# Second modulation's broadcasts made in column tiles and spread by DMA, a new order of the dense work, and two batches of the head's matmuls moved

## The chip, the core and the metric

The kernel runs on one core of one Trainium2 chip. The metric is device time in microseconds (us) for one execution of the whole program. A core has TensorE (PE in the profile: matmuls, with weight loads as PEld), VectorE (DVE), ScalarE (ACT), GpSimd (POOL) and SyncE (SP), each of which takes its own instructions in order; nearly all DMAs of this kernel are issued from SP's queue.

## The reference

One transformer-like block with adaptive layer norm. `c` gives six vectors of 512; the first three modulate the attention half, the last three the token-mixing half. Shapes: S = 2048 tokens, D = 512, 32 heads of 16, window 256, F = 1792.

```python
mod = (_silu(c) @ w_mod).reshape(c.shape[0], 6, 1, -1)
sa, ca, ga, sb, cb, gb = (mod[:, n] for n in range(6))
h = _layernorm(x) * (1 + ca) + sa
x = x + ga * A(h, wqkv, wo)          # causal attention, window 256, then @ wo
h = _layernorm(x) * (1 + cb) + sb
x = x + gb * B(h, w1, b1, w2, b2)    # layernorm, then an MLP over the 2048 tokens:
                                     # gelu(h^T @ w1 + b1) @ w2 + b2, transposed back
```

(`...copy()` and the batch dimension of 1 are left out.)

## The kernel before

Tokens are handled in 16 blocks of 128, four blocks to a token group (tg 0 to 3). There are three stages.

*Head* (first exponential at 12.54 us). x and the first third of `w_mod` are loaded; four blocks are normalised (`ln1_apply`, L258) and turned by PE into PSUM banks of pool `hpt` (`turn`, L544; banks for 128-column chunks `dc` 0/2 and 1/3). `fm(k)` (L530) is a batch of eight one-column matmuls that gives the scale and shift of the first modulation; `fm(0, 1, 2)` stands between `turn(1)` and `turn(2)`, `fm(3)` after `turn(3)`. DVE adds 1 (`modFM`, L556), and ACT and DVE modulate from PSUM into `h1T` (L562, L564), in two column parts. Then the first q and k are made (L579, L583, L587).

*Attention* (12.5 to 158.9 us). 76 units (tg, g8, ui): g8 is one of four groups of eight heads, ui a piece of the window (four pieces in tg 0, five after). Each unit has two exponentials on ACT (`emit_exp`, L649), which read scores that PE makes (L626, masks L638). When a (tg, g8) is through, PE multiplies by the values (`emit_av`, L666, reading `VaugT` and its half-swapped copy `Vx`), and DVE and POOL normalise (L677 to L701). Between these stand the *dense groups*, each of four 512-column matmuls and an evacuation on DVE: `q..`, `k..` (L354), `v..` (L331), `wo..` (attention output, L421), `bias`, and `bc..` (the broadcasts, L396). Names carry the token group and head group (`k10`: tg 1, g8 0) or the block (`v6`). Where a dense group is not ready, PE makes partial sums of the MLP's first product (`part_group`, L462), which the last stage then need not make. Only two PSUM banks (`ps_dn`) serve all of these.

The order is decided when the program is built: class `Plan` keeps a clock for each engine with fixed costs for each step (`g.us`, `cost`, `issue(t, cost)` for SP), takes the first name in the string `ORDER` that is ready by that clock, and emits instructions accordingly (`run_dense`, `force`, `drain`, `fill`). `force(needs(u + 1))` makes sure that q and k of the next unit are emitted before its scores. `PLAN` holds six margins. `at_unit` issues one background load per unit (`loads`): `w_mod` for the later modulations, `wo`, zeros for two of the k buffers, then `w1`.

For k of g8 2 and 3 (`copied`), DVE writes a plain copy `k`, and eight small DMAs (L378) put it into the zeroed `KT`. Values are swapped by two DMAs per pair of blocks (`swap`, L322). `h1T` of tg 1 to 3 is turned by DMA (`dma_start_transpose`, L310) and modulated in SBUF. Every DMA shares SP's queue.

The second modulation's vectors (and `ga`) are needed on all 128 partitions: `bc_group(v, ...)` multiplies `sT_rep` (silu of c, repeated over 128 columns, L593) by 512 columns of `w_mod`, four matmuls for each of the four vectors, and DVE casts each into its own tile (L403, L405). After `bc_ga`, four `fold_wod` (L957) multiply it into `wo`. `wo` groups need the folds, `bc_cb1` and `bc_sb`.

*Tail* (158.9 us to the end). `sum_up` (L1106) finishes six of the 14 F-chunks, the last four blocks get `wo` (`t_wo`, L1127) and the second modulation (t1 to t3, blocks `hb` 12 to 15; ACT L1145, DVE L1135 to L1154), L1203 finishes the other eight chunks, and L1227 is the second product `py`, 252 matmuls, with its epilogue.

Of the kernel before, what the change touches and what calls it, by code (L numbers as in the profile page):

```python
# [1 line left out]

# [6 lines left out]
DT = mybir.dt  # L9
# [3 lines left out]
P = 128  # L13
S = 2048
D = 512
# [13 lines left out]
def kernel(  # L29
# [63 lines left out]
    bc_cb1 = const.tile([P, D], DT.bfloat16, name="bc_cb1")  # L93
    bc_sb = const.tile([P, D], DT.bfloat16, name="bc_sb")
    bc_gb = const.tile([P, D], DT.bfloat16, name="bc_gb")
# [4 lines left out]
    bc_ga = modw.tile([P, D], DT.bfloat16, name="bc_ga")  # L100
# [27 lines left out]
    sT_rep = modw.tile([P, ND, P], DT.bfloat16, name="sT_rep")  # L128
# [199 lines left out]

    def v_group(tg, tl):
        def mm(pv, dc):  # L330
            nc.tensor.matmul(  # L331
                pv[:], lhsT=h1T[tg][:, dc, tl * P : (tl + 1) * P],
                rhs=wqkv[:, dc, 2 * D : 3 * D], start=(dc == 0), stop=(dc == ND - 1),
            )

        def evac(pv):
            nc.vector.tensor_copy(
                out=v_heads(tg % 3, tl, 0, H)[:, :, 0:DH], in_=pv[:].rearrange("p (h d) -> p h d", d=DH),
            )
# [8 lines left out]
    def qk_group(tg, g8, kind):  # L348
# [10 lines left out]
        def evac(pq):  # L359
            if kind == "q":  # L360
                QT[tg][g8] = qpool.tile([P, 4 * P], DT.bfloat16, name=f"QT{g8}")
                nc.vector.tensor_copy(out=QT[tg][g8][:], in_=pq[:])
                return
# [24 lines left out]
            ND, mm, evac, 1.35 if masked else 0.65,  # L388
# [5 lines left out]
    def bc_group(v, dst, add1, then=()):  # L394
        def mm(ps_b, k):
            nc.tensor.matmul(  # L396
                ps_b[:], lhsT=sT_rep[:, k, :], rhs=wmod_of(v)[:, k, :],
                start=(k == 0), stop=(k == ND - 1),
            )

        def evac(ps_b):
            if add1:
                nc.vector.tensor_scalar_add(out=dst[:], in0=ps_b[:], scalar1=1.0)  # L403
            else:
                nc.vector.tensor_copy(out=dst[:], in_=ps_b[:])  # L405
        return Group(ND, mm, evac, 0.65, [("w", v)] + [("w", "o")] * (v == 2), ("bc", v), then=then)
# [86 lines left out]
    with tc.manual_schedule():  # L493

        with tc.tile_pool(name="modps", bufs=1, space=bass.MemoryType.PSUM) as modps, tc.tile_pool(
            name="hpt", bufs=2, space=bass.MemoryType.PSUM
# [10 lines left out]
            st_ps = modps.tile([P, ND], DT.bfloat16, name="st_ps")  # L507
            nc.tensor.transpose(st_ps[:], c4[:], identity[0:ND, 0:ND])
# [9 lines left out]
            nc.scalar.activation(out=sig[:], in_=st_ps[:], func=ACT.Exp, scale=-1.0)  # L518
# [5 lines left out]
            nc.vector.tensor_tensor(out=sT[:], in0=st_ps[:], in1=sig[:], op=ALU.mult)  # L524
# [14 lines left out]
            banks = [hpt.tile([P, 2, 4 * P], DT.bfloat16, name="dn") for _ in range(2)]  # L539
            pts = [banks[dc % 2][:, dc // 2, :] for dc in range(ND)]  # L540

            def turn(tl):
                for dc in range(ND):
                    nc.tensor.transpose(  # L544
                        pts[dc][:, tl * P : (tl + 1) * P], xn1[0, tl][:, dc * P : (dc + 1) * P], identity[:]
                    )

            turn(0)
# [3 lines left out]
            fm(0, 1, 2)  # L552
# [5 lines left out]
            def modulate(dc, c0, c1, act):  # L558
                out, src = h1T[0][:, dc, c0:c1], pts[dc][:, c0:c1]
                scale, shift = modFM[:, 4 + dc : 5 + dc], modFM[:, dc : dc + 1]  # L560
                if act:
                    nc.scalar.activation(out=out, in_=src, func=ACT.Identity, bias=shift, scale=scale)  # L562
                else:
                    nc.vector.tensor_scalar(out=out, in0=src, scalar1=scale, scalar2=shift, op0=ALU.mult, op1=ALU.add)  # L564
# [28 lines left out]
            nc.gpsimd.tensor_copy(out=sT_rep[:], in_=sT[:].unsqueeze(2).to_broadcast([P, ND, P]))  # L593
# [112 lines left out]
        def ln23(tb):  # L706
# [21 lines left out]
            def modulate(by, op):  # L728
                return lambda eng: eng.tensor_tensor(out=v["h2"][:], in0=v["h2"][:], in1=by[:], op=op)
# [10 lines left out]
        BC = ((2, bc_ga, False), (4, bc_cb1, True), (3, bc_sb, False), (5, bc_gb, False))  # L740

        def bc(v, dst, add1):
            return bc_group(v, dst, add1, [
                (lambda g=g: fold_wod(g), 0.33, 0.1, ("fold", g)) for g in range(ND)
            ] if v == 2 else ())
# [4 lines left out]
            v1 k20 wo3 q31 v2 q10 q22 k21 q33 wo11 wo6 v0 q02 wo0 q21 k11 q30 k10 bc2 v3 k01 v7  # L750
            v6 v15 wo8 q01 q20 bias k33 q32 v10 k13 wo7 wo9 q03 v4 v8 q11 v5 k02 wo5 k12 v9 k31
            v14 q23 bc3 v13 wo2 k30 bc0 q13 v12 wo10 k22 v11 bc1 wo1 q12 wo4 k32 k23 k03
        """

        def make(name):
            kind, n = name.rstrip("0123456789"), name.lstrip("abciokqsvw")
# [6 lines left out]
            return bc(*BC[int(n)]) if kind == "bc" else bias_group()  # L763

        dense = [make(name) for name in ORDER.split()]
        PLAN = (0.2, 8.0, 5.0, 0.4, 0.6, 0.2)
# [9 lines left out]
        ready["w", "b"], pl.sp = 8.0, 5.0  # L776
# [51 lines left out]
        def drain():  # L828

            while pl.urgent:  # L830
# [3 lines left out]
                pl.dve = max(pl.dve, at) + cost  # L834
# [24 lines left out]
        def step():  # L859
# [5 lines left out]

            def then():
                if g.gives:
                    if g.lag:
                        evens.add(g.gives)
                        both = [("k", g.gives[1], n) for n in (2, 3)]  # L870
                        if all(k in evens for k in both):
                            ready[both[0]] = ready[both[1]] = ready[both[0][:2]] = issue(pl.dve, g.lag)
                    else:
                        ready[g.gives] = pl.dve + 0.1
                    kind, *_, tb = g.gives if g.gives[0] == "v" else ("", 0)
                    if kind:
                        if ("v", tb ^ 1) in ready and (tb % 4 < 2 or tb < 8):
                            ready["vx", tb ^ 1] = ready["vx", tb] = issue(pl.dve, 1.3)
                if g.then:
                    add_chain(g.then, pl.dve + (PLAN[2] if g.then[0][3] else 0.1))  # L880
            pl.urgent.append((pl.pe + 0.2, g.cost, b, g.evac, then))
# [74 lines left out]
        def fold_wod(g):  # L956
            nc.vector.tensor_tensor(out=wod[:, g, :], in0=wod[:, g, :], in1=bc_ga[:], op=ALU.mult)  # L957

        def at_unit(tg, ul, u, t):
# [45 lines left out]
        end, scored, pl.pe = 0.0, 0.6, 0.4  # L1005
# [13 lines left out]
        for u, (tg, g8, ui) in enumerate(units):  # L1019
            half = lambda v: 0.06 + 0.00166 * columns(units[v][0], units[v][2])  # L1020
            emit_exp(u, 0)
            start = max(end, scored)
            end = start + 2 * half(u)
# [14 lines left out]
            due(u + 1, end)  # L1038
            until = end if late or u + 1 in values_at else end - 1.3 if u == last else max(end, scored) + half(u + 1) + 0.1
            run_dense(until)  # L1040
            emit_exp(u, 1)
            if late:
                pl.pe = max(pl.pe, end + 0.05)
                emit_scores(u + 1, (1,))
                pl.pe += 0.37
                until = max(end, scored) + half(u + 1) + 0.1
# [11 lines left out]
        emit_av(NG - 1, ND - 1, (4,), False, True)  # L1058
        norm_out(0)
# [61 lines left out]
    with tc.tile_pool(name="xp2", bufs=4) as xp2, tc.manual_schedule():  # L1121
# [28 lines left out]
        def t2(tb):  # L1150
            h2 = hb[tb]
            t_apply(h2[:], xres[tb][:], (2, tb))
            nc.vector.tensor_tensor(out=h2[:], in0=h2[:], in1=bc_cb1[:], op=ALU.mult)
            nc.vector.tensor_tensor(out=h2[:], in0=h2[:], in1=bc_sb[:], op=ALU.add)  # L1154
# [118 lines left out]
```

## Time and profile before

| what | value |
|---|---|
| median of three runs | 248.73 us (248.49 to 249.42) |
| the profiled execution | 249.06 us, of which its span 247.3 us |
| granted TensorE clock | 1.00 in every stretch |
| head, 0 to 12.5 us | PE busy 9.52, DVE 9.08, ACT 3.59 |
| tg 0, 22.7 to 44.0 us | 21.3 us: ACT busy 20.92, DVE 19.69, PE 18.76 |
| first half of tg 1, 44.0 to 65.4 us | 21.4 us: ACT busy 18.61, PE 19.64, DVE 18.33 |
| 65.4 to 158.9 us | 93.5 us: ACT busy 92.91, PE 90.66, DVE 83.64 |
| start of the tail, 158.9 to 182.8 us | 23.9 us: PE busy 23.90, DMA 395 GB/s |
| last product, 182.8 to 247.3 us | 64.5 us: PE busy 61.56 |

A row of busy times by stretch is read against the stretch's length: an engine whose busy time equals it is what the stretch waits for. In the attention stage that is ACT, in the tail PE. "Busy" of PE counts overlapping matmuls once.

### The profile page before, as it was taken

Reading aid. Unit: us, or ns where it says so; the run is one execution under the profiler, and the core shown is the slowest. Engines: PE = TensorE matmul, PEld = TensorE weight load, DVE = VectorE, ACT = ScalarE, POOL = GpSimd, SP = SyncE. Lnnn points to the kernel's source line nnn. Section 1 sums busy time; section 2 is a strip of 40 time slices with the busy share of each in tenths; the row PEclk is TensorE's granted clock in tenths of the full one; section 3 lists DMA queues with packets and bytes.
Section 4 is the critical chain, followed back from the end, with each engine's and each line's share of the span. In section 5 each row is a group of like instructions: output and inputs, shape, how many; then the busy total and the mean of one; then the engine's idle time right before and its main releaser. Section 6 shows DMA issues by size and latency. Waiting matters only on the chain.

```text
span 247.3 us, 8336 instructions
## 1 busy us (share of the span) xinstructions
PE 233.0 (94%) x3599; PEld 119.7 (48%) x3599; DVE 180.4 (73%) x359; ACT 160.0 (65%) x183; POOL 109.6 (44%) x230
## 2 busy tenths in 40 slices
PE   6898897998899999899999999999999999999995
PEld 2643644544545545545545545544444444444444
DVE  6797999987799798989899999879724404241544
ACT  2395999997899999999999999713574400000000
POOL 6625551217647638875867888537600000000000
PEclk9999999999999999999999999999999999999999
DMA  6977994153640244000239500499970000201031
GB/s 192 332 243 184 160 297 149 24 133 67 178 155 5 52 88 87 11 3 3 52 64 302 159 3 5 150 357 415 409 310 0 0 0 5 82 21 64 24 106 44
DMA packets 32121, 30.49 MB, mean 123 GB/s; under 512 B 16212, under 2 KB 26708, under 8 KB 32084
## 3 DMA queue, kind: packets, MB, share of 16 engines
q1 hardware_dynamic: 32076, 29.96, 40.5%
q8 instruction: 28, 0.46, 0.8%
q14 instruction: 9, 0.07, 0.1%
q10 hardware_dynamic: 8, 0.00, 0.0%
HBM read 22.03 MB, written 2.10 MB: 98 GB/s over the span
## 4 chain that ended last, share of the span: by engine, by line
PE 58%; ACT 26%; DVE 9%; SPq 3%; issue 1%; POOL 1%; DMA 1%; ACTq 0%; POOLq 0%
ACT et L649 26%; PE py L1227 20%; PE pu L1106 8%; PE pss L626 6%; PE pu L1203 5%; PE dn L354 4%; PE dn L331 4%; PE dn L462 4%; SPq L378 3%; PE pss L638 2%; DVE ln_stats L242 2%; DVE KT L384 2%; PE pa L1127 1%; PE dn L421 1%; PE pss L666 1%
## 5 line engine op out<-in xcount | busy, mean ns | idle before, releaser
L649 ACT ACTIVATE et<-pss 128x1024 bf16<-128x1024 f32 (+1 forms) x152 | 139.6, 1039 | 7.0 <-PE pss L638 6.6
L1227 PE MATMUL py<-guT,w2r 128*128 128x512 bf16 (+2 forms) x252 | 48.6, 355 | 0.0
L626 PE MATMUL pss<-QT,KT 32*128 32x64 bf16 (+3 forms) x720 | 37.4, 254 | 4.4 <-ACT et L649 2.1
L1227 PEld LDWEIGHTS <-w2r 128*128 128x128 bf16 x252 | 23.6, 98 | 25.2
L1234 DVE SCALAR_TENSOR_TENSOR o<-py,bFM,bc_gb 128x512 bf16<-128x512 f32 (+2 forms) x18 | 11.9, 687 | 30.0 <-PE py L1227 30.0
L354 PE MATMUL dn<-h1T,wqkv 128*128 128x512 bf16 x120 | 32.6, 381 | 0.5 <-DVE KT L384 0.5
L626 PEld LDWEIGHTS <-KT 32*128 32x128 bf16 x720 | 14.3, 92 | 34.2 <-issue 22.5
L223 POOL TENSOR_SCALAR ln_ve<-ln_mv 128x1 f32<-128x1 f32 (+2 forms) x40 | 9.2, 230 | 41.1 <-DVE ln_mv L243 18.6
L677 DVE STREAM_TRANSPOSE t<-pss 128x512 f32<-128x512 f32 x32 | 20.9, 691 | 5.3 <-PE pss L666 5.3
L666 PE MATMUL pss<-et,VaugT 64*32 64x320 bf16 (+4 forms) x720 | 20.9, 253 | 1.1 <-ACT et L649 0.6
L666 PE MATMUL pss<-et,Vx 64*32 64x320 bf16 (+4 forms) x720 | 21.0, 254 | 0.7 <-DMA Vx<-VaugT 0.7
L693 POOL TENSOR_TENSOR merge<-t,zr 128x512 bf16<-128x512 f32 x13 | 13.8, 1059 | 15.7 <-DVE zr L690 15.7
L638 PE MATMUL pss<-mask_rown,mask_hown 32*128 32x128 bf16 (+1 forms) x304 | 20.7, 206 | 0.0
L666 PEld LDWEIGHTS <-VaugT 64*32 64x32 bf16 x720 | 18.9, 91 | 3.8 <-issue 3.3
L638 PE MATMUL pss<-mask_rfar,mask_hfar 32*128 32x64 bf16 (+1 forms) x304 | 19.9, 200 | 0.0
L226 POOL TENSOR_TENSOR ln_rb<-ln_ve,mhalf 128x1 f32<-128x1 f32 x32 | 18.4, 574 | 2.7
L666 PEld LDWEIGHTS <-Vx 64*32 64x32 bf16 x720 | 17.9, 91 | 2.2 <-DMA Vx<-VaugT 0.9
L331 PE MATMUL dn<-wqkv,h1T 128*128 128x512 bf16 x64 | 17.0, 381 | 1.0 <-DVE KT L384 0.9
L1114 DVE TENSOR_TENSOR gelu_a<-pu,part 128x512 f32<-128x512 f32 x10 | 6.4, 685 | 12.5 <-PE pu L1203 8.2
L462 PE MATMUL dn<-hb,w1hi 128*128 128x512 bf16 x56 | 15.1, 381 | 0.0
L354 PEld LDWEIGHTS <-wqkv 128*128 128x128 bf16 x120 | 9.6, 97 | 10.3 <-DVE KT L384 0.7
L421 PE MATMUL dn<-wod,OTd 128*128 128x512 bf16 x48 | 12.6, 381 | 0.0
(131 smaller groups left out, 368.3 us busy)
## 6 DMA issues: line engine op xcount, KB each, us to landing
w2r<-in_B_w_dram SPq DMA_DIRECT2D x14, 512.0 KB, 10.2
wmod<-in_w_mod_dram SPq DMA_DIRECT2D x12, 256.0 KB, 4.4
w1b<-in_B_w_dram SPq DMA_DIRECT2D x6, 448.0 KB, 5.9
Vx<-VaugT SPq DMA_DIRECT2D x16, 147.5 KB, 2.5
x<-in_A_x_dram SPq DMA_DIRECT2D x16, 128.0 KB, 4.6
w1hi<-in_B_w_dram SPq DMA_DIRECT2D x6, 320.0 KB, 5.0
out_dram<-otile SPq DMA_DIRECT2D x15, 128.0 KB, 1.7
wqkv<-in_B_w_dram SPq DMA_DIRECT2D x4, 320.0 KB, 3.3
```

What stands on the lines that cost most here:

```text
L226: nc.gpsimd.tensor_tensor(out=r, in0=ve[:], in1=mhalf[:, 0:n], op=ALU.pow)
L331: nc.tensor.matmul(pv[:], lhsT=h1T[tg][:, dc, tl * P : (tl + 1) * P], rhs=wqkv[:, dc, 2 * D : 3 * D], start=(dc == 0), stop=(dc == ND - 1),)
L354: nc.tensor.matmul(pq[:], lhsT=wqkv[:, dc, col0 : col0 + P], rhs=h1T[tg][:, dc, :], start=(dc == 0), stop=(dc == ND - 1),)
L421: nc.tensor.matmul(pa[:], lhsT=OTd[tg][g][:, tl * P : (tl + 1) * P], rhs=wod[:, g, :], start=(g == 0), stop=(g == ND - 1),)
L462: nc.tensor.matmul(ps[:], lhsT=w1_of(s0 + n, fc), rhs=hb[s0 + n][:], start=(n == 0), stop=(s0 + n + 1 == s1),)
L626: nc.tensor.matmul(pss[j // 2][:, j % 2, 64 * at : 64 * (at + c1 - c0)], lhsT=Kring[kh // 8 % 3][rows, g8, kh % 8].rearrange("p n t -> p ( ...
L638: nc.tensor.matmul(o[:, at[0] : at[-1] + 1 : step, :], lhsT=mask_h[name][rows].rearrange("p n t -> p (n t)"), rhs=mask_r[name][rows, :].un ...
L649: nc.scalar.activation(out=state["e", tg, g8, ui][:, 2 * a : 2 * a + 2, 0:n], in_=state.pop((u, a))[:, :, 0:n], func=ACT.Exp, scale=SCORE_ ...
L666: nc.tensor.matmul(state["po"][32 * j : 32 * j + 32, par, 64 * c0 : 64 * c1], lhsT=v[:, h * DV : h * DV + 32], rhs=state["e", tg, g8, ui][ ...
L677: nc.vector.transpose(out=state["t2"][:, par, :], in_=state["po"][:, par, :])
L1106: nc.tensor.matmul(pu[fc][:], lhsT=w1_of(sc, fc), rhs=hb[sc][:], start=(sc == done.get(fc, 0)), stop=(sc == NT - 1),)
L1227: nc.tensor.matmul(pys[n][:, c0:c1], lhsT=w2r[:, fc, tb * P : (tb + 1) * P], rhs=guT[fc][:, c0:c1], start=(fc == gelus[0]), stop=(fc == ge ...
```

## The change

1. One `bc` group in place of four. Its four steps each issue four matmuls of 32 columns of weights, one per vector, at `tile_position=(0, 32n)`; the four results land on partitions 32n of one PSUM bank. One DVE instruction adds 1 to the rows of `cb` and casts; one DMA takes partitions 0, 32, 64 and 96 to a DRAM tile `bc_rows`, a second one spreads that to `bc_all` on all partitions. `sT_rep` shrinks to 32 columns per chunk. Two small memsets on POOL are new. The group needs all of `w_mod` (and `wo`) and comes once; the folds follow it.
2. The planner: SP's cost of a load is 1.0 in place of 0.6; start values and margins of `PLAN` differ; a group with `PLAN[6]` could be evacuated on ACT, but `PLAN[6]` is empty, so no instruction moves there. Loads left at the end of the units are issued in one go.
3. `ORDER` is new throughout. The groups of tg 0 come as v0 v1 q01 v3 v2 k01 k02 q02 k03 q03 (before: v1 v2 v0 q02 v3 k01 q01 bias q03 k02 k03). The first ones of tg 1 come as v4 v7 q10 v5 k10, then `bc`, k11 v6 q11 k12 k13 (before: bc0, q10 k11 k10 bc2 v7 v6 k13 v4 q11 v5 k12). As built, `part_group` has 84 matmuls (before 75), `sum_up` 80 (88), the last chunks 60 (61).
4. In the head, `fm(0, 1)` goes ahead of `turn(0)`, and `fm(2)` stays between `turn(1)` and `turn(2)`. The pool `hpt` has a third bank, which takes the first three blocks of chunk 3, so that chunks 1 and 3 no longer share a bank there. The transposed `c` uses one of the three in place of a bank of its own.

```diff
-    sT_rep = modw.tile([P, ND, P], DT.bfloat16, name="sT_rep")
+    sT_rep = modw.tile([P, ND, 32], DT.bfloat16, name="sT_rep")
+
+    bc_row = modw.tile([P, D], DT.bfloat16, name="bc_row")
+    add_row = modw.tile([P, 1], DT.float32, name="add_row")
+    nc.gpsimd.memset(add_row[:], 0.0)
+    nc.gpsimd.memset(add_row[32:64, :], 1.0)
...
-    def bc_group(v, dst, add1, then=()):
+    BC = (2, 4, 3, 5)
+
+    def bc_group(then):
+
         def mm(ps_b, k):
-            nc.tensor.matmul(
-                ps_b[:], lhsT=sT_rep[:, k, :], rhs=wmod_of(v)[:, k, :],
-                start=(k == 0), stop=(k == ND - 1),
-            )
+            for n, v in enumerate(BC):
+                nc.tensor.matmul(
+                    ps_b[32 * n : 32 * n + 32, :], lhsT=sT_rep[:, k, :], rhs=wmod_of(v)[:, k, :],
+                    start=(k == 0), stop=(k == ND - 1), tile_position=(0, 32 * n), skip_group_check=True,
+                )
 
         def evac(ps_b):
-            if add1:
-                nc.vector.tensor_scalar_add(out=dst[:], in0=ps_b[:], scalar1=1.0)
-            else:
-                nc.vector.tensor_copy(out=dst[:], in_=ps_b[:])
-        return Group(ND, mm, evac, 0.65, [("w", v)] + [("w", "o")] * (v == 2), ("bc", v), then=then)
+            nc.vector.tensor_scalar_add(out=bc_row[:], in0=ps_b[:], scalar1=add_row[:])
+            dma.dma_start(out=bc_rows[:], in_=bc_row[0:P:32, :])
+            dma.dma_start(out=bc_all[:], in_=bc_rows[:].unsqueeze(0).to_broadcast([P, 4, D]))
+        return Group(ND, mm, evac, 0.65, [("w", v) for v in BC] + [("w", "o")], ("bc",), us=0.27, then=then)
...
-            banks = [hpt.tile([P, 2, 4 * P], DT.bfloat16, name="dn") for _ in range(2)]
-            pts = [banks[dc % 2][:, dc // 2, :] for dc in range(ND)]
+            banks = [hpt.tile([P, 2, 4 * P], DT.bfloat16, name="dn") for _ in range(3)]
+
+            def pt(dc, c0, c1):
+                n = 2 if dc == 3 and c1 <= 3 * P else dc % 2
+                return banks[n][:, dc // 2, c0:c1]
...
+            fm(0, 1)
             turn(0)
             ln1_apply(0, 3)
             build_masks()
             turn(1)
-            fm(0, 1, 2)
+            fm(2)
             turn(2)
             turn(3)
             fm(3)
...
-            v1 k20 wo3 q31 v2 q10 q22 k21 q33 wo11 wo6 v0 q02 wo0 q21 k11 q30 k10 bc2 v3 k01 v7
-            v6 v15 wo8 q01 q20 bias k33 q32 v10 k13 wo7 wo9 q03 v4 v8 q11 v5 k02 wo5 k12 v9 k31
-            v14 q23 bc3 v13 wo2 k30 bc0 q13 v12 wo10 k22 v11 bc1 wo1 q12 wo4 k32 k23 k03
+            v0 v4 wo7 k20 v7 k32 v12 wo5 q31 q10 v5 bc wo2 v1 wo6 v10 k21 k10 wo10 q01 v3 v2 k30
+            k22 v9 q20 wo8 k01 k23 k11 wo1 v8 v6 wo0 wo4 q33 q30 wo3 v11 q32 v15 q11 k02 v14 q23
+            wo11 q21 q22 k12 k13 q02 k03 q12 q03 k31 v13 k33 bias wo9 q13
...
-        PLAN = (0.2, 8.0, 5.0, 0.4, 0.6, 0.2)
+        PLAN = (0.2, 8.0, 3.0, 0.8, 0.0, 0.2, ())
...
-        ready["w", "b"], pl.sp = 8.0, 5.0
+        ready["w", "b"], pl.sp, pl.dve = 8.0, 5.6, 1.4
...
+                    if g.gives == ("bc",):
+                        issue(pl.dve, 0.65)
+                        pl.sp += 2.0
+                        landed = issue(pl.dve, 0.65) + 0.5
+                        for v in BC:
+                            ready["bc", v] = landed
+                        add_chain(g.then, ready["bc", 2])
+                        return
...
-                ready[key] = issue(t, 0.6) + 1.0
+                ready[key] = issue(t, 1.0) + 1.0
```

More of the change, by code (lines that the diff above doesn't have):

```diff
@@ L864, in step @@
                 return
+            over = pl.pe + 0.2
             def then():
@@ L1004 @@
         last = len(units) - 1
-        end, scored, pl.pe = 0.0, 0.6, 0.4
+        pl.end, pl.half, scored, pl.pe = 0.0, None, 0.6, 0.4
         values_at = {}
@@ L1021 @@
             emit_exp(u, 0)
-            start = max(end, scored)
-            end = start + 2 * half(u)
+            start = max(pl.end, scored)
+            pl.half, pl.end_of = start + half(u), half(u)
+            pl.end = start + 2 * half(u)
             if u == 0:
@@ L1058 @@
         emit_av(NG - 1, ND - 1, (4,), False, True)
+        while loads:
+            o, i, key = loads.pop(0)
+            dma.dma_start(out=o, in_=i)
         norm_out(0)
```

77 lines of the change are left out of this document (44 added, 33 removed).

## The prediction

> **What bounds the kernel now.** I read four views: busy time by stretch, the chain of work that ended last, what the exponentials (ACT, L649) waited for, and SP's queue around the longest such wait. Busy time by stretch first (columns: PE, PEld, DVE, ACT, POOL, granted clock, DMA share, GB/s):
>
> ```profile
> 22.70:44.00 21.30, 18.76 (x459) 10.47 (x457) 19.69 (x37) 20.92 (x25) 8.33 (x14) 1.00 0.79 188
> 44.00:65.40 21.40, 19.64 (x401) 10.05 (x408) 18.33 (x35) 18.61 (x20) 9.00 (x16) 1.00 0.35 75
> 65.40:158.90 93.50, 90.66 (x2059) 49.25 (x2067) 83.64 (x159) 92.91 (x100) 67.81 (x114) 1.00 0.28 77
> 158.90:182.80 23.90, 23.90 (x201) 11.21 (x186) 16.44 (x37) 8.95 (x12) 10.95 (x28) 1.00 1.02 395
> ```
>
> From 65.4 to 158.9 us ACT is busy 92.91 of 93.50: the attention stage cannot end earlier than its exponentials allow, so PE time saved there buys nothing by itself; it can only be spent on partial sums, which shorten the tail. In the tail PE has no gap. ACT has room only before 65.4. The chain of waits names where (start, length, what):
>
> ```profile
> 8.62 0.47 PE dn L544 x8
> 9.09 0.19 PE ps_fm L530 x8
> 9.31 0.18 DVE modFM L556
> 9.51 1.75 DVE h1T L564 x5
> ...
> 20.10 1.41 DVE KT L384 x2
> 21.51 0.61 DVE QT L362
> 22.16 0.40 PE pss L626 x8
> 22.56 0.14 PE pss L638 x8
> 22.70 6.79 ACT et L649 x8
> ```
>
> ACT's timeline gives the size of each wait in brackets:
>
> ```profile
> 12.54 7.16 ACT L649 ACTIVATE et<-pss 128x1024 bf16<-128x1024 f32 x8 [0.26 <-PE pss L638]
> 22.68 20.91 ACT L649 ACTIVATE et<-pss 128x1024 bf16<-128x1024 f32 x24 [2.98 <-PE pss L638]
> 43.98 14.86 ACT L649 ACTIVATE et<-pss 128x1024 bf16<-128x1024 f32 x16 [0.38 <-PE pss L638]
> 60.61 3.77 ACT L649 ACTIVATE et<-pss 128x1024 bf16<-128x1024 f32 x4 [1.78 <-PE pss L638]
> 65.40 1.02 ACT L649 ACTIVATE et<-pss 128x1024 bf16<-128x1024 f32 x1 [1.01 <-PE pss L638]
> ```
>
> So ACT loses 2.98 us at unit 4 (22.68), 0.38 at unit 16, the first of tg 1 (43.98), 1.78 and 1.01 at units 24 and 26 (60.61, 65.40). The last two are SP's: its queue runs without a gap from 47.4 to 66.3 us:
>
> ```profile
> 47.37 2.53 SPq L310 DMA_TRANSPOSE h1T<-xn  x2
> 49.99 1.17 SPq L322 DMA_DIRECT2D Vx<-VaugT  x2
> 51.26 2.56 SPq L310 DMA_TRANSPOSE h1T<-xn  x2
> 53.91 1.18 SPq L322 DMA_DIRECT2D Vx<-VaugT  x2
> 55.20 8.12 SPq L378 DMA_DIRECT2D KT<-k  x8
> ```
>
> The last `Vx` lands at 58.75 and the values' matmuls start at 58.80; the last k copy lands at 64.96 (issued 62.71), the exponential starts 0.44 later. Two of the eight issues took 1.84 us, the others some 0.6; both fell on an instruction fetch.
>
> **Part by part.** Each term is in us of ACT's or PE's path; the profiled run (249.06 us, span 247.3) lies 0.33 over the median of 248.73, and I apply the differences to the median.
>
> *A, the head: −0.55.* The chain goes turn(3), `fm(3)`, `modFM`, `h1T`. `fm(0, 1)` leaves the place ahead of turn(2): 16 of the 24 matmuls that take 0.58 there, 0.39 us. It runs earlier, where PE idles for `xn` (sT is done at 6.75, the block of turn(0) at 7.27). turn(3) cannot start before its own `xn` at 8.24; then 0.47 + 0.19, so `modFM` at about 8.9 in place of 9.31, −0.4. The third bank adds a little: ACT waits 0.61 for DVE's `h1T` (10.18 to 10.79) because chunks share a bank; without it QT is copied earlier, but DVE's own five h1T and six KT steps remain: −0.15. Bounds −0.3 (the bank gives nothing, 8.24 slips by 0.1) and −0.7.
>
> *B, unit 4: −0.6.* There `k01` (two evacuations, 1.41) and then `q01` (0.61) stand between PE and the scores. In the new order q01 comes before k01, with as many groups ahead of them; q01's evacuation then lies beside k01's matmuls and 0.61 leaves the chain. Bounds −0.6 and 0 (DVE late by another step).
>
> *C, unit 16: +1.3.* `k10` was fourth among the first groups of tg 1 with bc0, q10, k11 ahead; now v4, v7, q10, v5 are ahead. Its evacuation (1.41) and the scores (0.54) follow. One more group is 4 × 0.216 = 0.86 of PE and one more evacuation 0.68 on DVE, and v4 to v7 need `h1T` of tg 1; 0.86 to 1.54 of it shows, less what PE is earlier by A and B no longer hides. I take +1.3 between +0.7 and +1.9. A and B are about given back here.
>
> *bc itself.* PE: 16 matmuls at 4.5/16 = 0.28 busy, 0.216 a piece when streamed, 3.45 us; now 16 of 32 columns, four beside each other. The nearest row is the values' matmuls (64*32 tiles), of which eight with 320 columns start within 58.80 to 58.95, the time of one: four passes of 0.216, 0.9 us. 2.6 us of PE is freed, and goes to partial sums. Four casts of 0.69 on DVE become one, −2.1 of DVE in a stage where it has 1.6 to 3.1 spare: worth nothing by itself. SP gains two issues and a hold: the second DMA waits for the first to land. Stores of 64 to 128 KB land 1.5 to 1.7 after issue, so SP is held about 1.6, and everything behind it: one zeroing load, four transposes (1.27 each), the last `Vx`, the k copies, w1hi. Bounds of the hold: 1.5 (those stores) and 6.0 (the zeroing loads, 256 KB, which shared the engines with wmod). I take 1.6, as 4 KB is nearer to the stores. The folds wait for `bc_all`: nothing but `wo` waits for them, half a unit group later.
>
> [...]
>
> *D, units 24 and 26: −1.3.* In the new order SP reaches bc's evacuation at about 44.4 us; 0.6 of issue, 1.6 hold, 0.6 of issue, 0.7 zeroing, 4 × 1.27, 1.2 for Vx: 54.0, where the k copies could start, 1.2 before 55.20. By DVE they start as late as 55.20 + 1.3 (C) − 0.86 (one group fewer ahead of k12) = 55.6. From 54.8: seven issues of 0.65, one or two long ones (+1.25 each), 2.25 to land: 62.9 to 64.1; + 0.44, against 65.40: −2.0 to −0.9 at that point, middle −1.45, of which A, B, C make +0.15; that would be −1.6. I take −1.3, since Vx's wait (1.78) also hangs on v-evacuations that C delays. Bounds −2.8 (both waits go) and +0.6 (as late as before and C in full).
>
> *E, 65 to 159 us: +0.5.* The w1hi and wqkv loads of the late partial sums were issued at 129.4, behind tg 3's k copies (122.3 to 128.0), and landed by 133.4; the changed order makes sums of eight matmuls a chunk from unit 63 on, and four Vx and eight copies stand ahead of their loads. ACT has 0.59 to lose in this stretch now; 0 to +1.2.
>
> *F, the tail: −1.3.* `sum_up` and the last chunks issue 80 + 60 matmuls in place of 88 + 61: 9 × 0.216 = −1.94. But block 15's modulated rows must be there for them: ACT ends it at 180.56, and PE first needs it at 182.77 − 6 × 0.216 = 181.47, a slack of 0.9. With 1.94 gone PE would ask at 179.5; a leftover step of DVE (0.41 at 166.07) disappears from that chain, so it is ready at 180.15: 0.65 of the 1.94 is lost. Bounds −1.94 and −0.9.
>
> Sum: −0.55 − 0.6 + 1.3 − 1.3 + 0.5 − 1.3 = −1.95: **246.8 us**, own range 245.8 to 247.9.
>
> **Rivals.**
> - *The full gain*: q10 and k10 meet a PE already early, C is 0.7, E is 0, F −1.94, D −1.3: −0.55 − 0.6 + 0.7 − 1.3 − 1.94 = −3.7, 245.0. For it: DVE loses three casts. Against: k10 is plainly behind more v groups.
> - *New waits take it back*: C 1.9, E 1.2, B −0.3: −0.55 − 0.3 + 1.9 − 1.3 + 1.2 − 1.3 = −0.35, 248.4. For it: ACT is the bound to 0.6 us over 93.5, so every new wait there counts in full.
> - *Slower: SP held by the round trip through DRAM.* bc_rows is issued right behind a zeroing load; if it lands like that load, 6.0 after issue, the hold is 4.4 longer, the transposes of tg 1, Vx and the k copies are that much later, and the last copy lands at 63.5 + 4.4 − 0.8 (start by SP's 54.0 in place of 54.8) = 67.1; + 0.44 is 2.1 past 65.40. D is then +1.95 in place of −1.3: 250.1; with v7's and k11's groups late as well (h1T of tg 1 by as much), up to 251. It decides from the point where D passes +0.65, a hold some 2.7 longer, 4.3. Against: the stores.
> - *The column tiles do not overlap*, and bc takes up to 3.45 of PE just before tg 1's k11 and v6: C + 1.9, and 2.6 us (12 matmuls) fewer partial sums are possible in the same time: 246.8 + 1.9 = 248.7. Against it: the values' matmuls. [...] No row of the profile has four tiles with all 128 rows.
>
> **How the numbers follow.** Forecast 0.42; full gain 0.15; new waits 0.21; SP held 0.17; no overlap 0.05. What a measurement of this kernel can tell from no change is about 0.5%, 1.24 us: faster is under 247.49, slower over 249.97. Of the forecast's own range 0.32 of its 0.42 is faster, with the full gain's 0.15 and a 0.03 of the new waits 0.50; SP held is slower (0.17) and 0.02 of the new waits, with C at its end and D at zero; the rest, 0.31, is no change. The range: 245.0 at the full gain; up to 250.1, SP held.
>
> **What would show it.** First exponential at about 12.0; unit 4's wait 2.4; a new wait of 1 to 2 us at the first unit of tg 1; SP idle 1.6 between bc's two DMAs; the last k copy of tg 1 landing at 63 to 64; the four bc matmuls of a step starting together; a short wait of PE for block 15 at the end of `sum_up`. It is wrong if the first wait of tg 1 is 3 us or the hold 4, or if a wait opens that I did not name, in tg 2 or 3, where I worked out no unit singly.

## The result: 0.6 to 0.9% slower, and a profile that does not show it

The changed kernel takes 250.68 us (median of 14 executions, 248.73 to 253.62) against 248.55 (14 executions, 247.99 to 249.42). The ratio, from which the one execution in the slower state (253.62) is left out, is 1.0064, 95% interval 1.0039 to 1.0089 (the two medians alone give 1.0086); a second series of 12 gave 1.0086 (1.0056 to 1.0116). The forecast was 246.8, with a range of 245.0 to 250.1.

The profiled execution of it took 249.06 us with a span of 247.3, exactly what the profiled execution of before took. Neither is typical: that of before is 0.5 over its median, that of the changed kernel 1.6 under. So the difference of the two traces is not the difference of the two kernels, and it took further profiles to see it. What the first pair does show is each term of the sum. ACT's timeline of the changed kernel (start, length; in brackets the wait ahead):

```profile
12.38 3.56 ACT L666 ACTIVATE et<-pss 128x1024 bf16<-128x1024 f32 x4
...
22.07 20.86 ACT L666 ACTIVATE et<-pss 128x1024 bf16<-128x1024 f32 x24 [2.38 <-PE pss L655]
44.51 14.87 ACT L666 ACTIVATE et<-pss 128x1024 bf16<-128x1024 f32 x16 [1.59 <-PE pss L655]
60.29 3.77 ACT L666 ACTIVATE et<-pss 128x1024 bf16<-128x1024 f32 x4 [0.91 <-PE pss L655]
65.37 27.95 ACT L666 ACTIVATE et<-pss 128x1024 bf16<-128x1024 f32 x30 [1.31 <-PE pss L655]
94.13 65.50 ACT L666 ACTIVATE et<-pss 128x1024 bf16<-128x1024 f32 x70 [0.81 <-PE pss L655]
```

Unit 4's wait is 0.60 shorter (2.98 before), unit 16's 1.21 longer (0.38), units 24 and 26 wait 2.22 together (2.79), and unit 41 has a new wait of 0.81. SP's queue in the same execution, where I had put one of the two largest gains:

```profile
44.65 0.58 SPq L417 DMA_DIRECT2D bc_rows<-bc_row  x1
46.33 0.35 SPq L418 DMA_DIRECT2D bc_all<-bc_rows  x1
46.72 1.35 SPq L1026 DMA_DIRECT2D KT<-zero  x1
48.26 7.17 SPq L316 DMA_TRANSPOSE h1T<-xn  x4
55.54 1.17 SPq L328 DMA_DIRECT2D Vx<-VaugT  x2
57.23 6.17 SPq L388 DMA_DIRECT2D KT<-k  x8
```

The hold for the round trip is no longer than forecast: 1.68 us from the start of the first bc DMA's issue to the start of the second's, where the sum counted 0.6 and 1.6. But the four transposes take 7.17 us in place of 5.1, and the k copies start at 57.23 and not at 54.8. POOL's timeline says why:

```profile
53.26 0.95 POOL L240 TENSOR_SCALAR xn<-x,norm 128x512 bf16<-128x512 bf16 x1 [8.87 <-DMA h1T<-xn]
```

The fourth `xn` has no free buffer (pool `xp` has three), so POOL stands until the first transpose has read the first one. That transpose, issued at 48.26, lands at 53.07, behind `bc_all` (512 KB, landed 51.78) and the zeros (52.46). Only then can the fourth `xn` be written and the fourth transpose be issued, at 54.24.

The tail behaved: the chain of waits at its end, first in the changed kernel, then its last row in before:

```profile
181.32 1.46 PE pu L1144 x6
182.78 12.95 PE pu L1241 x60
195.73 48.43 PE py L1265 x252
```

```profile
195.94 48.43 PE py L1227 x252
```

The attention stage ended 0.75 us later than before (159.62 against 158.87), and `py` started 0.21 earlier.

### The profile page after: what moved, and what is told of

It is laid out like the page before. It is cut to its first block, busy times and chain, and to the rows that moved or that the text cites. A ratio compares the mean times of both kernels' runs of the same rounds, so it can differ in the third digit from the quotient of the medians.

```text
span 247.3 us, 8344 instructions
## 1 busy us (share of the span) xinstructions
PE 232.2 (94%) x3599; PEld 118.9 (48%) x3599; DVE 178.0 (72%) x354; ACT 159.9 (65%) x183; POOL 111.8 (45%) x234
## 4 chain that ended last, share of the span: by engine, by line
PE 51%; ACT 25%; DVE 11%; DMA 5%; SPq 4%; issue 2%; POOL 2%; POOLq 0%; DVEq 0%
ACT et L666 25%; PE py L1265 20%; PE dn L364 6%; PE pss L643 5%; PE pu L1241 5%; PE dn L475 4%; PE dn L341 3%; DMA wqkv<-in_A_wqkv_dram 2%; PE pu L1144 2%; SPq L388 2%; PE pss L655 2%; DVE KT L394 2%; DMA Vx<-VaugT 2%; PE pss L683 2%; PE dn L434 2%
## 5 line engine op out<-in xcount | busy, mean ns | idle before, releaser
L643 PE MATMUL pss<-QT,KT 32*128 32x64 bf16 (+3 forms) x720 | 38.8, 254 | 5.7 <-ACT et L666 3.2
L1272 DVE SCALAR_TENSOR_TENSOR o<-py,bFM,bc_all 128x512 bf16<-128x512 f32 (+2 forms) x18 | 11.9, 688 | 30.0 <-PE py L1265 30.0
L643 PEld LDWEIGHTS <-KT 32*128 32x128 bf16 x720 | 15.2, 92 | 36.0 <-issue 24.3
L364 PE MATMUL dn<-h1T,wqkv 128*128 128x512 bf16 x120 | 31.5, 381 | 0.5 <-DVE KT L394 0.2
L655 PE MATMUL pss<-mask_rown,mask_hown 32*128 32x128 bf16 (+1 forms) x304 | 21.4, 206 | 0.0
L655 PE MATMUL pss<-mask_rfar,mask_hfar 32*128 32x64 bf16 (+1 forms) x304 | 20.6, 200 | 0.0
L746 POOL TENSOR_TENSOR hb<-hb,bc_all 128x512 bf16<-128x512 bf16 x15 | 17.7, 1181 | 2.0 <-DVE hb L746 0.7
L710 POOL TENSOR_TENSOR merge<-t,zr 128x512 bf16<-128x512 f32 x11 | 11.7, 1063 | 13.0 <-DVE zr L707 13.0
L475 PE MATMUL dn<-hb,w1hi 128*128 128x512 bf16 x60 | 16.2, 381 | 0.0
L240 POOL TENSOR_SCALAR xn<-x,norm 128x512 bf16<-128x512 bf16 x12 | 10.0, 839 | 12.4 <-DMA h1T<-xn 12.4
```

What stands on the lines that cost most here:

```text
L364: nc.tensor.matmul(pq[:], lhsT=wqkv[:, dc, col0 : col0 + P], rhs=h1T[tg][:, dc, :], start=(dc == 0), stop=(dc == ND - 1),)
L475: nc.tensor.matmul(ps[:], lhsT=w1_of(s0 + n, fc), rhs=hb[s0 + n][:], start=(n == 0), stop=(s0 + n + 1 == s1),)
L643: nc.tensor.matmul(pss[j // 2][:, j % 2, 64 * at : 64 * (at + c1 - c0)], lhsT=Kring[kh // 8 % 3][rows, g8, kh % 8].rearrange("p n t -> p ( ...
L655: nc.tensor.matmul(o[:, at[0] : at[-1] + 1 : step, :], lhsT=mask_h[name][rows].rearrange("p n t -> p (n t)"), rhs=mask_r[name][rows, :].un ...
```

## What differs between executions: the granted clock

Each execution comes with its mean granted TensorE clock. The 26 executions of the changed kernel in two series:

| mean clock | executions | median us |
|---|---|---|
| 0.998 to 1.0 | 8 | 249.5 |
| 0.992 to 0.993 | 12 | 250.5 |
| 0.985 to 0.986 | 6 | 252.3 |

Within a row the times still spread by about 3 us (248.73 to 251.59 at full clock), so the clock is one part of it. Of 104 executions of before, in the four series of the experiments, 98 have 0.998 or more. Experiments 1 to 4, 5 to 8, 9 to 12 and 13 to 15 form four series, each on another chip; the six executions of before with less are 1 of 29, 1 of 29, 4 of 23 and 0 of 23 in them, so shares are best compared within a series. By an estimate from the 3.4 us at 0.50 in the profile of experiment 6 (kernel b, below), one such stretch takes 0.007 off the mean clock (1.7 of 247 us) and two take 0.014, which are the steps of the table. The first profile of the changed kernel, itself at clock 1.0, shows where such a stretch can come from. Busy time by stretch, first the changed kernel, then before (columns: PE, PEld, DVE, ACT, POOL, clock, DMA share, GB/s):

```profile
30.10:33.50 3.40, 1.74 (x50) 1.06 (x35) 3.08 (x7) 3.40 (x5) 1.79 (x4) 1.00 1.06 357
89.70:93.10 3.40, 1.95 (x24) 0.84 (x24) 3.26 (x7) 3.40 (x4) 3.40 (x4) 1.00 1.07 189
```

```profile
30.10:33.50 3.40, 2.99 (x105) 1.81 (x86) 3.36 (x7) 3.40 (x5) 2.28 (x4) 1.00 0.97 314
```

At 30 us, before ran a bc group in these gaps and dense groups beside it. The single bc group of the change needs all of `w_mod` and comes at 42.4, tg 0's dense groups are done, and nothing is ready: PE is busy 1.74 of 3.40 us. At 89.7 it is 1.95; the lowest such stretches of before, its first and last 5 us left out, have 2.33 (18.8 us) and 2.34 (96.9 us).

## Experiments

Times are against before in the same series; "dip" is a mean clock under 0.995.

**1. The changed kernel again.**

> The changed kernel itself, once more. The profiled execution of it took 249.06 us, while its 14 timings have a median of 250.68 and run from 248.73 to 253.62; before runs from 247.99 to 249.42. Theory 1 (some wait on a DMA is longer in most executions than in the profiled one): this profile is of an execution of 250 to 252 us, and a wait of ACT or PE on a DMA is 1 to 3 us longer than in the first profile. Theory 2 (the clock granted to TensorE dips in some executions): the waits are the same as in the first profile, and the extra time lies in a stretch whose granted clock is under 1.

250.23 us (249.44 to 252.73); 9 of 12 executions with a dip. The profile fell on one at clock 1.0 and has the waits of the first (units 24 and 26: 0.97 and 1.67, k copies from 57.94). Theory 2 fits a part of the spread; but the sum of the two waits is itself longer than in the first profile, and grew to 1.28 and 2.13 in a later one (kernel a of experiments 5 to 7). Both vary.

**2. Only ga's row spread at once.**

```diff
-            dma.dma_start(out=bc_all[:], in_=bc_rows[:].unsqueeze(0).to_broadcast([P, 4, D]))
+            spread(0, 1)
+            unspread.append((1, 4))
...
         dma.dma_start_transpose(out=h1T[tg][:, :, tl * P : (tl + 1) * P], in_=xn1[tg, tl][:])
+        if tl == 3:
+            spread_rest()
```

> The changed kernel, but only the row of ga (128 KB) is spread at once; the other three rows (384 KB) are spread by a DMA behind the four transposes of tg 2's h1T. Theory 1 (the 512 KB of bc_all, with the zeros behind it, delay the first transpose's landing to 4.8 us; POOL waits for that landing before it can write the fourth xn, and so the fourth transpose is issued 2.1 us late): POOL's wait falls by 1 to 2 us, the k copies of g8 2 and 3 start at 55.5 to 56.5 in place of 57.2, and the time falls by 0.5 to 1.5 us against the changed kernel. Rival (the transposes are late because of the zeros alone, or the k copies are set by DVE): the start of the k copies and the time are as in the changed kernel within 0.4 us.

249.95 us, ratio 1.0048 (1.0019 to 1.0077). The four transposes take 5.40 us in place of 7.17, POOL's wait for the buffer falls from 8.87 to 6.75 and the k copies start at 55.26: the 512 KB were what made the first transpose late enough to hold up the fourth. Seven of 12 still have a dip, and the time is 0.3 to 0.7 under the changed kernel, which the intervals do not tell apart.

**3. The head's edits alone, on before.**

```diff
+            fm(0, 1)
             turn(0)
...
-            fm(0, 1, 2)
+            fm(2)
```

(and the third bank of `hpt`)

> The kernel before with the head's edits alone (fm(0, 1) ahead of turn(0), the third bank); the order of the dense work is the old one. Theory (the load of wqkv, which lands at 10.07 in the changed kernel, takes the place of modFM as what the first q and k wait for): the first exponential at 12.3 to 12.45 in place of 12.54, and 0.0 to 0.3 us of the whole time. Rival (my prediction): first exponential at 12.0, and the whole time 0.5 lower, since the planner's order is the same.

249.02 us, ratio 1.0016 (0.9991 to 1.004): no gain. First exponential at 12.51. The reason I gave in advance, wqkv's load, is not what this profile shows: here `fm(0, 1)` starts late, at 7.32 (see 10). It is what the first profile of the changed kernel shows, where the chain runs through that load's landing at 10.07.

**4. The old order in the changed kernel**, with `bc` for bc0 and the other three left out.

```diff
-            v0 v4 wo7 k20 v7 k32 v12 wo5 q31 q10 v5 bc wo2 v1 wo6 v10 k21 k10 wo10 q01 v3 v2 k30
+            v1 k20 wo3 q31 v2 q10 q22 k21 q33 wo11 wo6 v0 q02 wo0 q21 k11 q30 k10 v3 k01 v7
...
```

> The changed kernel with the old order string (bc where bc0 stood, the other three bc left out); column tiles, DRAM round trip and head stay. Theory (the order is what costs: k10 behind four groups, the late Vx of tg 2): unit 16's wait falls from 1.59 to under 0.8, and the time is 1 to 2 us under the changed kernel's 250.7. Rival (the round trip costs): the time stays at 250 to 251.5 us and the waits at units 24 and 26 are as long as in the changed kernel or longer.

262.21 us, ratio 1.0535 (1.0492 to 1.0579). Unit 16's wait is gone, as expected, and unit 4's is back at 2.98, so both come from the order; but this order, run through the changed planner, has a wait of its own on k copies in tg 2, so the gain of 1 to 2 us that I expected was not put to the test and the order is not priced. It does show the clock. PE's timeline, then the stretches:

```profile
107.37 0.42 PE L643 MATMUL pss<-QT,KT 32*128 32x320 bf16 x1 [4.89 <-DMA KT<-k]
```

```profile
102.50:107.30 4.80, 0.00 (x0) 0.00 (x0) 4.76 (x11) 0.59 (x1) 4.28 (x6) 0.78 0.23 42
107.40:110.00 2.60, 2.04 (x25) 0.69 (x33) 2.41 (x7) 0.24 (x1) 2.06 (x7) 0.50 0.15 26
110.00:113.50 3.50, 2.80 (x112) 2.01 (x96) 2.86 (x7) 2.38 (x3) 2.86 (x8) 0.50 0.02 5
113.50:117.00 3.50, 3.45 (x27) 1.42 (x27) 2.54 (x5) 3.10 (x4) 3.33 (x5) 0.50 0.02 5
```

PE is idle for 4.89 us; the clock falls to half within it and is still there in the last of these rows, up to 117.0 us.

**5 to 7. The half-idle stretches filled.** Spare matmuls of 512 columns whose results are never read: between 30.5 and 33.5 us (a: `warm_dn(n)` issues n of them into a free bank, but nothing while a dense group is in progress), four ahead of the wo group at 92.2 us (b), or both. The theory of the clock was that these stretches bring the lower mean clocks (18 of the 26 executions above are at 0.993 or less), so that those executions go when the stretches are filled. For a, three calls ask for six (a third call, with one, stands behind the second half of unit 8's scores), as the expectation says; the traces show three (in a from 32.5 us on), some 0.65 us of PE.

```diff
             run_dense(until)
+            if u in (8, 9):
+                warm_dn(u - 6)
...
             if self.at == 0:
+                if self.gives in (("wo", 5),):
+                    for _ in range(4):
+                        nc.tensor.matmul(self.ps[:], lhsT=identity[:], rhs=wqkv[:, 0, 0:D], start=True, stop=True, skip_group_check=True)
```

> The changed kernel with six spare matmuls (512 columns, 1.3 us, results never read) between 30.5 and 33.5 us, where PE is busy 1.74 of 3.40 us in its profile and 2.99 in that of before, which ran bc's matmuls there. [...]

> The changed kernel with four spare matmuls (0.86 us) ahead of the first matmul of the wo group that waits for Vx at 92.2 us, in the second stretch in which PE is busy little (1.95 of 3.40 us from 89.7). Theory of the clock: fewer executions with 0.986 and 0.993 than in the changed kernel, about as many gone as with the first stretch filled, median 249.5 to 250. Rival (late DMA): no change.

> The changed kernel with both stretches filled. Theory of the clock: nearly all executions at a clock of 0.998 or more, as before, and a median of 249.0 to 249.6, which is what its executions without a dip have (249.48 over 8); the spread falls from 4 us to under 2. Rival: as the changed kernel.

| kernel | median us | ratio (95%) | executions with a dip |
|---|---|---|---|
| a | 249.91 | 1.0056 (1.0025 to 1.0086) | 2 of 12 |
| b | 251.37 | 1.0114 (1.0077 to 1.0150) | 5 of 6 |
| both | 249.85 | 1.0034 (1.0011 to 1.0057) | 3 of 12 |

Filling the stretch at 30 us takes most of the dips away; filling the other alone, in the same series, does not. Three forecasts failed: a dip to 0.986 is left in a, where I had expected none, the spread of "both" is still 4.9 us and not under 2, and b's median did not fall. Kernel b's profile caught a dip:

```profile
30.50:33.90 3.40, 1.81 (x57) 1.09 (x39) 3.10 (x7) 3.40 (x5) 1.16 (x3) 0.95 0.96 309
33.90:35.00 1.10, 0.71 (x18) 0.62 (x19) 1.04 (x2) 1.10 (x3) 1.00 (x2) 0.50 1.06 330
35.00:36.00 1.00, 0.99 (x3) 0.44 (x3) 0.00 (x0) 1.00 (x2) 0.39 (x2) 0.50 0.96 307
36.00:37.00 1.00, 1.00 (x7) 0.15 (x9) 0.47 (x1) 0.46 (x1) 0.00 (x0) 0.52 1.05 350
37.00:38.00 1.00, 1.00 (x41) 0.63 (x41) 0.96 (x3) 0.53 (x1) 0.00 (x0) 1.00 0.89 306
```

The clock is 0.50 from about 33.6 to 37.0, right behind the half-idle stretch: 3.4 us, and ACT then waits 1.01 us at unit 12. The two other profiles with a dip, those of experiments 10 and 4, have their first at the same place: from 34.4 to 37.8 us, behind a stretch in which PE was busy 1.64 of 3.40 us, and from 33.5 to 36.9, behind 1.99 of 3.40. For the executions without a profile it follows from most dips going away when the stretch is filled. But a's executions at full clock still run from 248.6 to 251.88: the clock is not all of it. The gain from filling is 0.6 us against the median of the changed kernel's 26 executions (250.5); the rows of the table above differ by 1.0 for one dip.

**8. Split and both fills.**

> Both stretches filled, and only ga's row spread at once, the other three rows behind the four transposes. If the two effects are separate they add: the profiled execution of the split alone was 248.07 at clock 1.0, so a median of 248.0 to 248.6, level with before or up to 0.5 us faster. If the split's gain was chance: 249.0 to 249.6.

249.49 us, ratio 1.0031 (1.0010 to 1.0052): the two gains did not add, and the time is where I had put it if the split's gain was chance. The trace shows why the split gains nothing: the transposes take 5.18 us, but the second DMA, 384 KB, now stands ahead of `Vx`, the k copies start at 57.19 and unit 24 waits 1.97. Two of 12 have a dip; those at full clock lie closer together (248.56 to 249.95) than with the fills alone (247.99 to 250.73).

**9. Before again.**

> The kernel before itself, for a second profile of it. The first one (249.06 us) is 0.5 over the median of its executions, and its first exponential is at 12.54 us; eight profiles of the changed head lie between 11.97 and 12.97. Theory (the first profile of before caught a late fourth load of x or wmod in the head): first exponential at 12.0 to 12.2 and a time of 248.3 to 248.7. Rival (12.5 is where the old head always stands): 12.4 to 12.6.

248.12 us (one execution), and the first exponential at 12.60: the rival. The old head stands at 12.5 to 12.6 every time (four profiles: 12.44 to 12.64). What was unusual in the first profile of before are units 24 and 26: 1.25 and 0.54 here, 1.78 and 1.01 there.

**10. The old head in the changed kernel** (two banks again).

```diff
-            fm(0, 1)
             turn(0)
...
-            fm(2)
+            fm(0, 1, 2)
```

> The changed kernel with the head as before (turn(0) first, fm(0, 1, 2) between turn(1) and turn(2), two banks). Theory (with fm(0, 1) ahead of turn(0), a late load of wmod holds PE before turn(0); the fourth xn uses the buffer of the first and so waits for turn(0); fourth xn ends at 8.2 to 9.2 in the changed head): xn ends at 8.2 to 8.3 here, first exponential at 12.5 or less, median 0.0 to 0.5 under the changed kernel's 250.5. Rival (the head's edit gains what I predicted, 0.55): median 0.3 to 0.6 over it.

250.32 us, ratio 1.0078 (1.0049 to 1.0106): no difference that can be told from the changed kernel. Five of six have a dip. The fourth `xn` ends at 8.17 here, as expected. In the profiles with the new head and three buffers it ends at 8.21 to 9.21, and the first exponential is at 11.97 to 12.97. PE's timeline of "both" (experiment 7), where it came latest:

```profile
6.06 1.91 PE L531 MATMUL dn<-zero 128*128 128x512 bf16 x4
7.77 0.60 PE L548 MATMUL ps_fm<-sT,wmod 128*128 128x1 bf16 x16
8.23 0.61 PE L565 MATMUL dn<-identity,xn 128*128 128x128 bf16 x8
8.67 0.34 PE L548 MATMUL ps_fm<-sT,wmod 128*128 128x1 bf16 x8
```

The first row is the end of 12 warm-up matmuls (`warm(12)`) that stand ahead of `fm(0, 1)` and run from 2.68 to 7.97 here, past the start of the next row. `fm(0, 1)` starts at 7.77 (6.81 in the first profile of the changed kernel, where the 12 end at 6.50), and turn(0), for which everything was there at 7.3, stands behind it; the fourth `xn` starts at 8.72. The expectation blamed `wmod`'s load; here it is these 12, which took 4.1 to 5.3 us from profile to profile. In others it is a load: `wmod`'s in the profile of experiment 1, `wqkv`'s in the first profile of the changed kernel.

**11. Four buffers for `xn`.**

```diff
-    xp = tc.alloc_tile_pool(name="xp", bufs=3)
+    xp = tc.alloc_tile_pool(name="xp", bufs=4)
```

(`plus`, 32 bytes, moves to the pool `modw` to make room, its two memsets with it; nothing else is edited.)

> The changed kernel with four buffers for xn in place of three. It takes away two waits at once: the fourth xn of the head no longer waits for turn(0), and in tg 1 POOL no longer waits for the first transpose to land before it writes the fourth xn. Theory: fourth xn in the head ends at 8.2 in every execution, first exponential at 11.9 to 12.2 unless PE itself stands behind wmod, transposes of tg 2 issued without the gap of 2.1 us, k copies starting at 55.0 to 56.0 in place of 57.2; median 0.6 to 1.2 under the changed kernel. Rival (these waits are hidden): within 0.3 of it.

248.05 us, ratio 0.9966 (0.9937 to 0.9995): 2.2 to 2.6 us under the changed kernel (2.3 under experiment 10 in the same series), the largest single effect and about twice the most that I had expected (1.2). SP's queue, then ACT's timeline from unit 24 on:

```profile
46.34 0.34 SPq L418 DMA_DIRECT2D bc_all<-bc_rows  x1
46.74 0.98 SPq L1026 DMA_DIRECT2D KT<-zero  x1
47.90 5.25 SPq L316 DMA_TRANSPOSE h1T<-xn  x4
53.25 1.17 SPq L328 DMA_DIRECT2D Vx<-VaugT  x2
54.96 5.61 SPq L388 DMA_DIRECT2D KT<-k  x8
```

```profile
59.81 31.79 ACT L666 ACTIVATE et<-pss 128x1024 bf16<-128x1024 f32 x34 [0.42 <-PE pss L655]
```

The transposes take 5.25 us and the k copies start at 54.96, right behind DVE's cast of k, which ends at 54.68. Unit 24 waits 0.42, unit 26 not at all. The transposes took 7.09 to 7.25 in all six profiles of the new order with three buffers and `bc_all` in one DMA, and 5.22 to 5.25 in all three with four. The first exponential did not gain (12.23 to 12.62 in four profiles): `fm(0, 1)` still stands behind the warm-up matmuls (until 7.60 here) or `fm` behind `wmod`. Eight of 12 executions have a dip, median 248.2; the other four 247.3.

**12. Four buffers, split and both fills.**

> Four buffers for xn, ga's row spread first, and both stretches of a half-idle PE filled with spare matmuls, in the changed kernel. If clock, spread and xn are the three causes and add: median 248.0 to 248.7, level with before or up to 0.5 us faster, and a spread under 2 us. If the new order itself costs: 249.0 to 249.6.

248.82 us, ratio 0.9997 (0.9976 to 1.0019), between the two expectations. None of 12 has a dip, against eight of 12 in experiment 11, in the same series. With the fourth buffer the split costs: its second DMA, 384 KB, goes ahead of `Vx`, and unit 24 waits 1.26 in place of 0.42.

**13, 14. Four buffers and the fills, without the split.** First both stretches, then the one at 30 us alone.

> Four buffers for xn and spare matmuls in both half-idle stretches; bc_all spread in one DMA as in the changed kernel. The executions of xn_4 whose clock stayed at 1.0 took 246.96 to 247.66 us, those with a dip 247.78 to 249.77. Theory (xn's buffer and the clock are the two causes, and the split, which puts 384 KB ahead of Vx, is what kept best3 at 248.8): hardly any dip, median 247.2 to 247.8, faster than before by 0.4 to 0.6%. Rival (the spare matmuls themselves cost as much as the dips): 248.0 to 248.9.

> As xn4_fill, but with only the stretch at 30 us filled, where before ran two of its four bc groups. Theory (this stretch is the main one: fill_30 had 10 of 12 executions without a dip, fill_90 one of 6): the same share without a dip as with both filled, within 2 of 12, and the same median within 0.3. Rival (each stretch does its part): about half of the executions at 0.991 to 0.993, median 0.3 to 0.6 over xn4_fill.

247.90 us, 0.9971 (0.9957 to 0.9986), one dip in 11; and 247.53 us (246.78 to 247.93), 0.9949 (0.9931 to 0.9968), no dip in 7. The second is the fastest kernel of the study, 1.1 us under before and about 3 under the changed one. The four matmuls at 92 us bring nothing that shows. Against 0.9966 with four buffers and eight dips in 12, both gain 0.4 us at most, and that on another chip.

**15. Before with four buffers.**

> The kernel before with four buffers for xn. If three buffers hurt the change alone (bc_all's traffic ahead of the transposes makes the first one land late): within 0.5 us of before. If the buffer helps any version of this kernel by as much (POOL and DVE wait 0.9 and 1.2 us for transposes there too): 1 to 2.5 us faster than before, and then the change itself gains nothing even with the buffer.

248.69 us, ratio 1.0007 (0.9991 to 1.0024). The buffer is worth nothing to the kernel before: there the transposes go in pairs with `Vx` between them and no bulk copy ahead. So the wait belongs to the change.

## Why the prediction was wrong

In executions at full clock: before 248.6, the changed kernel 249.5, with four buffers 247.3 (four executions; 247.5 to 247.9 in experiments 13 and 14). So the new order, head, tail and bc together gain 0.7 to 1.3 us; three buffers take back 1.6 to 2.2, and the dips another 0.6 to 1.0 in the median. That is a part of the 1.95 that the change was priced at, and two things that I did not name turn it round.

Of the seven signs that I had listed, five showed. The first exponential (12.38, not 12.0) and the last k copy of tg 1 (landed at 64.93, not 63 to 64) did not, and a wait that I had not named opened in tg 2 (unit 41), which I had given as a sign of being wrong.

- **D, the step that failed: "0.6 of issue, 1.6 hold, 0.6 of issue, 0.7 zeroing, 4 × 1.27, 1.2 for Vx: 54.0, where the k copies could start".** From 44.4 these terms come to 54.2. Hold, issues and zeros were right in sum: the transposes start at 48.26, where the terms ahead of them give 47.9. The "4 × 1.27" took SP's time for a transpose and left out what the fourth waits for: a buffer that is free only when the first has landed. In before the transposes take 3.1 us to landing (median of 12), and I did not ask what 768 KB ahead of them would do (4.8 for the first). The edit was priced as a hold of SP's queue and not as traffic. In place of −1.3, D came out at about +0.8: units 24 and 26 wait 2.1 to 3.4 together in the six profiles with three buffers and `bc_all` in one DMA (median 2.7), and 1.8 to 2.8 in the four with the old kernel's order (median 1.9). With a fourth buffer and no split the k copies start at 54.96 to 55.36, near where I had put them (54.8), and the waits at units 24 and 26 are 0.42 to 1.05 in all. The rival of the held SP named the right place, and nearly the right time (250.1), with the wrong cause, which is luck: the row landed within 1.7 us. It also took the transposes for those of tg 1; those are issued from 21.04 on, and the ones behind the hold are tg 2's.
- **bc: "2.6 us of PE is freed, and goes to partial sums".** The matmuls overlapped as forecast (16 in 1.05 us; forecast 0.9), and the partial sums came (84 in place of 75). But a hole opened at 30 us: from 28 to 36 us PE runs 8 dense matmuls of 512 columns, before 15, and four of the seven that are missing are a bc group's; the others the new order had through earlier. I read "granted clock 1.00 in every stretch" as a property of the kernel, when here it went with PE's busy share: 98 of 104 executions of before, with 2.33 of 3.40 us in the lowest stretch, are at 0.998 or more, and 8 of 26 of the changed kernel, with 1.74. The cost, 1.0 us between the rows of the clock table and 0.6 by filling the hole, had no term.
- **A, −0.55, mis-sized: about −0.1.** First exponential with the old head 12.44 to 12.64, with the new one 11.97 to 12.97 (median 12.5). "turn(3) cannot start before its own xn at 8.24" took that 8.24 as given, but the edit itself can move it: `fm(0, 1)` ahead of turn(0) hangs on the end of the warm-up matmuls and on the load of `wmod`, and the first q and k on that of `wqkv`. When all are early the gain is as predicted (11.97 and 11.98, forecast 12.0).
- **B right** (−0.60; −0.6). **C right** (+1.21; +1.3). The old order takes both away again (experiment 4).
- **E right in size, wrong in place**: +0.5 to +0.9 between unit 26 and the end of the exponentials in five of the six profiles, 1.8 in that of b (median 0.7; forecast +0.5), most of it the wait at unit 41. There PE stands 0.85 us for tg 2's `Vx` ahead of a wo group (92.21 to 93.06), and the scores are queued behind. The w1hi loads did not show.
- **F, −1.3; −0.96**: PE waits for block 15 as forecast (the chain goes through ACT's row for it, which ends at 181.3), a little longer.
- **The base.** D was sized on waits of 1.78 and 1.01 in a profile 0.5 us over its kernel's median. Two other profiles, of before again and of before with four buffers (248.12 and 248.08 us), show 1.25 to 1.31 and 0.53 to 0.54. There some 1.8 us was to be gained, not 2.8.

With the measured sizes the sum is −0.1 − 0.6 + 1.2 + 0.8 + 0.7 − 1.0 = +1.0 in place of −1.95; at full clock the executions differ by 0.9, and the dips come on top.

What stays open: how the effect of the buffer divides beyond the waits at units 24 and 26 (2.1 to 3.4 us with three buffers, 0.4 to 1.05 with four), what a dip costs apart from what else varies in the executions that have one, and why the second half-idle stretch, hardly busier than the first, makes few dips.

## What to carry to other kernels

A DMA put into a queue is costed three times: its issue, the wait that it needs, and its bytes ahead of what is issued behind it (here four transposes took 7.17 us behind 512 KB and 5.40 behind 128 KB, the zeros in both); then look for who waits for a landing to reuse a buffer. Work taken off an engine can leave a hole. Here PE went from 2.99 to 1.74 busy of 3.40 us at 30 us, 18 of 26 executions had a dip, and some 0.65 us of spare matmuls in that stretch left 2 of 12, where 5 of 6 in the same series had one without them (b). So look at the busy share over a few microseconds around such a place, not over the stage, and try what something put in is worth. And before differences of 1% are read from two traces, compare each profiled execution with the median and the clocks of its kernel's executions.

## What the hardware showed that I had not expected

The granted clock fell to 0.50 for 3.4 us after a stretch in which PE was busy 1.81 of 3.40 us, with no idle time over 0.7 us in it (profile of b; 1.64 of 3.40 us in that of experiment 10). The mean clock of the changed kernel's executions fits one or two such falls in 18 of 26 and none in the other eight; one of those eight is the first profile, which has a stretch like it (1.74 of 3.40 us) at clock 1.00. So a fall came behind a half-busy stretch in some executions and not in all, and 98 of 104 executions of before, whose first profile has 2.33 of 3.40 us in its lowest stretch (first and last 5 us left out), show none.

Four column tiles of 32 columns that use all 128 rows do overlap: 16 matmuls, each 0.38 us by its row, in 1.05 us. PE's timeline of the changed kernel:

```profile
42.44 1.05 PE L410 MATMUL dn<-wmod,sT_rep 128*32 128x512 bf16 x16
```

No row of before has such tiles; the values' matmuls, from which the prediction had worked out 0.9 us, use 64 rows.
